# Two blocks at a time through the product with w_in, in the seven-product form of Strassen's method

## The chip, the cores and the metric

The kernel runs on one core of one Trainium2 chip. The metric is the device time of one execution in microseconds (us), the median of several. A core has TensorE (PE in the rows; its weight loads, which overlap the matmuls, are PEld), VectorE (DVE), ScalarE (ACT), GpSimd (POOL) and SyncE (SP), which here issues all DMAs. Each engine works through its own instructions in the order in which the program gave them; semaphores between engines say when one may start.

## What is computed

An attention in windows of 32 queries, and two multilayer perceptrons behind it, all in float32:

```python
x = attention(q, k, v, mem_k, mem_v)          # 3072 tokens x 512
h = np.maximum(np.maximum(x @ w1, x @ w2), x @ w3)   # 512 -> 768
x = h @ w_out_1                                # 768 -> 512
h = x @ w_in                                   # 512 -> 2048
g = np.where(h >= 1, h, np.where(h <= -1, 0.0, (h + 1) ** 2 / 4.0))
out = g @ w_out                                # 2048 -> 512
```

The change touches `x @ w_in` and what stands around it.

## The kernel before

**Blocks and products.** The 3072 tokens are NB = 6 blocks of 512. Every float32 operand of a product is split into a high part that TensorE takes at its full rate (`hi`, type fp32r) and the rest (`lo`), and each product is three matmuls: hi with hi, hi with lo, lo with hi (`mm3`, L483). ScalarE casts the high part, GpSimd or VectorE subtracts to get the low one (`split`, L498, for the values between layers).

**Slots.** Work is in slots of 12 matmuls, 128x128 stationary, 512 columns moving, 4 chunks x 3 terms. `slot_l1` and `slot_l2` are the first perceptron, `slot_l3(i, f)` (L576) is unit f (128 of the 2048 columns) of x @ w_in for block i, with the function g behind it: ScalarE's relu (L584), VectorE's min-multiply (L585) and maximum with the bank (L586), then `split` (L501, L503). `slot_l4(i, f)` (L589) adds that unit's share of the product with w_out in four banks; after unit 15 the banks are copied out and stored. In slot_l3 the weights are the stationary operand, in slot_l4 the moving one.

**Order.** The order is written out by hand. Up to some 150 us a list (`PLAN`) mixes loads, attention and the first block. Then a loop over `order` runs the first perceptron of blocks 1 to 5, 24 slots a block; up to block 4 one step of attention follows each slot, and in a cycle of six slots (`BY_PART`, L637, `round_step`, L617) the weights of the second perceptron are fetched, rounded on ScalarE and VectorE (`abs_w` to `sum_w`, L132 to L148) and stored to a buffer in DRAM, `wd`. In the last block (no attention left) `w_step` (L639) loads them back in pairs of units (L178) and splits them (`split_w`, L184 on ScalarE, L185 on VectorE). The order of the units is `round2` (L103): c0 c1, c2 d0, c3 d1, c4 d2 and so on, c for w_in and d for w_out. The first four pairs go into a pool `w2` of eight tiles at the right end of the memory, opened when attention's pool is closed (L724), the other twelve into `wpool`, tile by tile as the first perceptron's weights fall free. Last, `orderB` (L712 to L715) alternates slot_l4 of one unit with slot_l3 three units on, block after block, 96 of each. Its inputs, the first perceptron's results, come back from the DRAM buffer `yd` (`load_y`, L561) and are split for the next block during this one (`split_y`, L572 on ScalarE, L573 on GpSimd).

**Banks and tiles.** Banks 0 to 3 collect slot_l4 (and slot_l2), banks 6 and 7 take turns for slot_l1 and slot_l3. Tags in the pools say which tiles share buffers: `st` (two of 8 KB a partition) for fetched weights, `c` (two of 4 KB) for rounding, loads of y and outputs, `xh` and `xl` (two of 8 KB each) for a block's split input, `hh` and `hl` (three of 2 KB each) for split values between layers.

Of the kernel before, what the change touches and what calls it, by code (L numbers as in the profile page):

```python
# [65 lines left out]
def attention_then_two_mlps(ctx, tc, q, k, v, mem_k, mem_v, w1, w2, w3, w_mid, w_in, w_out, out):  # L66
# [25 lines left out]
    wd = dram.tile([2 * K2, P, TB], F32, name="wd")  # L92
# [14 lines left out]
    Q1, Q2 = len(round1) // 2, len(conv) // 2  # L107
# [39 lines left out]
    def sum_w(q, c):  # L147
        nc.vector.tensor_tensor(out=c, in0=c, in1=staged.pop(q)[:, :, :, 0], op=ALU.add)  # L148
# [382 lines left out]
    def slot_l2(j, f):  # L531
        hi, lo = hs.pop(("A", j, f))
        whi, wlo = weights["b", f]
        for d in range(KD):
            c = slice(d * P, (d + 1) * P)
            mm3(acc[d], whi[:, c], wlo[:, c], hi, lo, f == 0, f == K1 - 1)
            if f == K1 - 1:
                if bp:
                    y = pair_or_y(d < 2, f"y_{j}_{d}")
                else:  # L540
                    y = mx.tile([P, TB], F32, tag=("hh", "hl")[d % 2], name=f"y_{j}_{d}", bufs=3)
                nc.scalar.copy(out=y, in_=acc[d])
                store = partial(nc.sync.dma_start, out=yd[d * P:(d + 1) * P, j * TB:(j + 1) * TB], in_=y)
                if bp:
                    store()
                else:
                    stores.append(store)

    yr, yh, yl, halves = {}, {}, {}, []

    def pair_or_y(paired, name):
        if not paired:
            return mx.tile([P, TB], F32, tag="y", name=name, bufs=2)
        if not halves:
            t = stage.tile([P, 2, TB], F32, tag="c", name=name, bufs=2)
            halves.extend(t[:, i] for i in range(2))
        return halves.pop(0)

    def load_y(i, h):
        yr[i, h] = stage.tile([P, 2, TB], F32, tag="c", name=f"yr{i}_{h}", bufs=2)  # L560
        nc.sync.dma_start(  # L561
            out=yr[i, h],
            in_=yd[2 * h * P:2 * (h + 1) * P, i * TB:(i + 1) * TB].rearrange("(k p) t -> p k t", p=P))

    def split_y(i, h):
        if h == 0:
            yh[i] = mx.tile([P, KD, TB], F32R, tag="xh", name=f"yh{i}")
            yl[i] = mx.tile([P, KD, TB], F32R, tag="xl", name=f"yl{i}")
        src = yr.pop((i, h))
        for k in range(2):  # L570
            kk = 2 * h + k
            nc.scalar.copy(out=yh[i][:, kk, :], in_=src[:, k])  # L572
            nc.gpsimd.tensor_tensor(  # L573
                out=yl[i][:, kk, :], in0=src[:, k], in1=yh[i][:, kk, :].bitcast(F32), op=ALU.subtract)

    def slot_l3(i, f):  # L576
        s = next_mm()
        whi, wlo = weights["c", f]
        for kk in range(KD):
            c = slice(kk * P, (kk + 1) * P)  # L580
            mm3(s, whi[:, c], wlo[:, c], yh[i][:, kk, :], yl[i][:, kk, :], kk == 0, kk == KD - 1)

        a = mx.tile([P, TB], F32, tag="t", name=f"u_{i}_{f}", bufs=2)
        nc.scalar.activation(out=a, in_=s, func=AF.Relu, bias=0.5, scale=0.5)  # L584
        nc.vector.scalar_tensor_tensor(out=a, in0=a, scalar=1.0, in1=a, op0=ALU.min, op1=ALU.mult)  # L585
        nc.vector.tensor_tensor(out=a, in0=s, in1=a, op=ALU.max)  # L586
        split(("B", i, f), a, f"b{i}_{f}")

    def slot_l4(i, f):  # L589
# [3 lines left out]
        for t in range(TB // P):  # L593
# [4 lines left out]
            if last:  # L598
                ob = pair_or_y(t % 2, f"ob{i}_{t}")
# [10 lines left out]
    bp = {}  # L610
# [6 lines left out]
    def round_step(acts):  # L617
        if "out" in acts and kept:
            q, c = kept.pop(0)
            n = 2 * (q - Q1)  # L620
            nc.sync.dma_start(out=wd[n:n + 2].rearrange("t p f -> p t f"), in_=c)
# [5 lines left out]
        if "b" in acts and q in tiles:  # L627
            sum_w(q, tiles[q])
            kept.append((q, tiles.pop(q).bitcast(F32)))
# [7 lines left out]
    BY_PART = "out in in", "", "", "a", "", "b"  # L637

    def w_step(room):  # L639
# [4 lines left out]
        if room > 0 and q < asked[0]:  # L644
            split_w(q, bp["w"] if q < Q1 + 4 else wpool)
            ready[0] += 1

    with tc.manual_schedule(engines={ENG.PE, ENG.DVE, ENG.Activation, ENG.Pool, ENG.SP}):
# [63 lines left out]
        orderB = [(slot_l3, 0, 0), (slot_l3, 0, 1), (slot_l2, NB - 1, K1 - 1), (slot_l3, 0, 2)]  # L712
        l3 = [(slot_l3, i, f) for i in range(NB) for f in range(K2)]
        l4 = [(slot_l4, i, f) for i in range(NB) for f in range(K2)]
        orderB += [s for a, b in zip(l4, l3[3:] + [None] * 3) for s in (a, b) if s]  # L715

        last_block = 0
        for s, (f, *a) in enumerate(order):
            j = a[0]
            if f is not slot_l2 and j == NB - 1 and last_block == 0:  # L720
# [3 lines left out]
                bp["w"] = ctx.enter_context(tc.tile_pool(name="w2", bufs=8, side="right"))  # L724
# [14 lines left out]
            if last_block:  # L739
# [3 lines left out]
                w_step(t - 2 * (ready[0] - Q1 - 4) - 3)  # L743
                if t in (8, 14):
                    split_y(0, t // 6 - 1)
                if t in (2, 8):
                    load_y(0, t // 6)
# [8 lines left out]
        for s, (f, *a) in enumerate(orderB):  # L756
            w_step(s > 2)
            if f is slot_l3:
                i, ff = a
                assert ("c", ff) in weights and ("d", max(ff - 2, 0)) in weights  # L760
            f(*a)
            if f is slot_l3 and i + 1 < NB:
                if ff in (5, 9):
                    split_y(i + 1, ff // 4 - 1)
                if ff in (1, 5):
                    load_y(i + 1, ff // 4)
# [30 lines left out]
```

## Time and profile before

| | us |
|---|---|
| median of three runs | 1052.25 (1051.94 to 1056.75) |
| the profiled execution, its own time | 1055.15 |
| its span, first to last instruction | 1053.3 |

| engine | busy us | share of the span |
|---|---|---|
| PE | 1027.2 | 98% |
| DVE | 456.7 | 43% |
| ACT | 350.1 | 33% |
| POOL | 227.7 | 22% |

A matmul's record lasts from its start to a modelled end, and records of neighbours overlap; what a matmul costs in a full queue is the distance from its start to the next one's. Busy shares of the whole span mix stages, so the rows below are read stage by stage: the first 150 us or so are loads and attention, 157 to 452 us the middle stage (first perceptron and attention), 452 to 519 us the last block of the first perceptron, and from there the second perceptron.

### The profile page before, as it was taken

To read this page: it belongs to the slowest core of one execution; us is meant where nothing else is said; L and a number is where in the kernel's file an instruction comes from. 1 tells how busy PE (TensorE), PEld (TensorE's weight loads), DVE (VectorE), ACT (ScalarE), POOL (GpSimd) and SP (SyncE) were. 2 spreads that over 40 slices of the span, in tenths; PEclk is the share of its full clock that TensorE was granted. 3 is DMA by queue.
4 is the path that set the end of the run, shared out by engine and by line. 5 is a ranking of instruction groups with operands and counts; after the bars stand their busy time and mean duration, and the time that the engine had idled before them with its cause. 6 is when DMAs were issued, how large, how long until landed. Compare 5 with 4: busy or idle time off the path is not lost.

```text
span 1053.3 us, 17983 instructions
## 1 busy us (share of the span) xinstructions
PE 1027.2 (98%) x7542; PEld 832.3 (79%) x7542; DVE 456.7 (43%) x733; ACT 350.1 (33%) x545; POOL 227.7 (22%) x172
## 2 busy tenths in 40 slices
PE   7799899999999999999999999999999999999998
PEld 5677678878877878888888888888888888888886
DVE  4699934466565565534332232232222223223222
ACT  5665533342333332333332222222222222222222
POOL 0023410100000000103123223323322322332221
PEclk9999999999999999999999999999999999999999
DMA  7866547557456445154210010010001001001001
GB/s 166 216 166 172 142 122 199 123 120 198 113 125 200 114 111 178 38 189 151 100 61 21 1 60 21 1 54 26 1 1 61 21 1 60 1 1 40 1 1 40
DMA packets 163808, 89.91 MB, mean 85 GB/s; under 512 B 126096, under 2 KB 143504, under 8 KB 163728
## 3 DMA queue, kind: packets, MB, share of 16 engines
q1 hardware_dynamic: 163728, 88.77, 30.6%
q8 instruction: 59, 0.97, 0.4%
q14 instruction: 21, 0.17, 0.0%
HBM read 67.76 MB, written 20.97 MB: 84 GB/s over the span
## 4 chain that ended last, share of the span: by engine, by line
PE 87%; DVE 7%; DMA 3%; SPq 1%; issue 1%; ACT 1%; POOL 0%; DVEq 0%; POOLq 0%; ACTq 0%
PE bank L484 19%; PE bank L485 19%; PE bank L486 19%; PE bank L597 8%; PE bank L596 8%; PE bank L595 8%; DVE c L144 1%; PE bank L397 1%; DVE c L148 1%; PE bank L355 1%; DVE c L141 1%; SPq L243 1%; DMA kq<-in_k_dram 1%; DVE c L142 1%; PE bank L417 1%
## 5 line engine op out<-in xcount | busy, mean ns | idle before, releaser
L585 DVE SCALAR_TENSOR_TENSOR u<-u 128x512 f32<-128x512 f32 x96 | 71.2, 741 | 367.5 <-ACT u L584 367.5
L503 POOL TENSOR_TENSOR hl_b<-u,hh_b 128x512 fp32r<-128x512 f32 x96 | 123.8, 1290 | 373.9 <-ACT hh_b L501 256.0
L484 PE MATMUL bank<-xh,hi 128*128 128x512 f32 x432 | 174.9, 405 | 1.2 <-ACT xh L425 0.7
L486 PE MATMUL bank<-xh,lo 128*128 128x512 f32 x432 | 168.9, 391 | 1.8 <-POOL lo L173 1.8
L485 PE MATMUL bank<-xl,hi 128*128 128x512 f32 x432 | 169.0, 391 | 0.3 <-DVE xl L429 0.2
L484 PE MATMUL bank<-yh,hi 128*128 128x512 f32 x384 | 150.4, 392 | 0.0
L485 PE MATMUL bank<-yl,hi 128*128 128x512 f32 x384 | 150.2, 391 | 0.0
L486 PE MATMUL bank<-yh,lo 128*128 128x512 f32 x384 | 150.2, 391 | 0.0
L597 PE MATMUL bank<-hi,hl_b 128*128 128x512 f32 x384 | 150.0, 391 | 0.0
L596 PE MATMUL bank<-lo,hh_b 128*128 128x512 f32 x384 | 149.9, 390 | 0.0
L595 PE MATMUL bank<-hi,hh_b 128*128 128x512 f32 x384 | 149.8, 390 | 0.0
L584 ACT ACTIVATE u<-bank 128x512 f32<-128x512 f32 x96 | 57.6, 600 | 238.7 <-PE bank L486 220.1
L503 POOL TENSOR_TENSOR hl_a<-t,hh_a 128x512 fp32r<-128x512 f32 x34 | 47.0, 1382 | 338.2 <-ACT hh_a L501 292.3
L501 ACT CAST hh_b<-u 128x512 fp32r<-128x512 f32 x96 | 59.6, 621 | 147.8 <-DVE u L586 147.8
L486 PEld LDWEIGHTS bank<-xh,lo 128*128 128x128 f32 x432 | 81.1, 188 | 20.3 <-POOL lo L173 2.7
L484 PEld LDWEIGHTS bank<-xh,hi 128*128 128x128 f32 x432 | 81.2, 188 | 19.3 <-DVE t L519 1.2
L485 PEld LDWEIGHTS bank<-xl,hi 128*128 128x128 f32 x432 | 81.3, 188 | 15.9 <-DVE xl L429 1.0
L519 DVE TENSOR_TENSOR t<-bank,t 128x512 f32<-128x512 f32 x72 | 49.6, 689 | 85.7 <-PE bank L486 85.1
L485 PEld LDWEIGHTS bank<-yl,hi 128*128 128x128 f32 x384 | 72.2, 188 | 15.8
L486 PEld LDWEIGHTS bank<-yh,lo 128*128 128x128 f32 x384 | 72.1, 188 | 15.9
L484 PEld LDWEIGHTS bank<-yh,hi 128*128 128x128 f32 x384 | 72.1, 188 | 15.7
L595 PEld LDWEIGHTS bank<-hi,hh_b 128*128 128x128 f32 x384 | 72.1, 188 | 15.6
(88 smaller groups left out, 1247.0 us busy)
## 6 DMA issues: line engine op xcount, KB each, us to landing
st<-in_moe_w_out_dram SPq DMA_DIRECT2D x22, 512.0 KB
st<-in_moe_w_dram SPq DMA_DIRECT2D x18, 512.0 KB
vw<-in_v_dram SPq DMA_DIRECT2D x152, 56.0 KB
st<-in_moe_w_in_dram SPq DMA_DIRECT2D x16, 512.0 KB
wd<-c SPq DMA_DIRECT2D x16, 512.0 KB
w<-wd SPq DMA_DIRECT2D x16, 512.0 KB
yd<-y SPq DMA_DIRECT2D x24, 256.0 KB
yr<-yd SPq DMA_DIRECT2D x12, 512.0 KB
```

What stands on the lines that cost most here:

```text
L141: V.tensor_scalar(out=cf, in0=cf, scalar1=LEAST, scalar2=MOST, op0=ALU.max, op1=ALU.min)
L484: nc.tensor.matmul(out, whi, xhi, start=first, stop=False)
L485: nc.tensor.matmul(out, whi, xlo, start=False, stop=False)
L486: nc.tensor.matmul(out, wlo, xhi, start=False, stop=last)
L501: nc.scalar.copy(out=hi, in_=h)
L503: e.tensor_tensor(out=lo, in0=h, in1=hi.bitcast(F32), op=ALU.subtract)
L519: nc.vector.tensor_tensor(out=cur["t", j, f], in0=s, in1=cur["t", j, f], op=ALU.max)
L584: nc.scalar.activation(out=a, in_=s, func=AF.Relu, bias=0.5, scale=0.5)
L585: nc.vector.scalar_tensor_tensor(out=a, in0=a, scalar=1.0, in1=a, op0=ALU.min, op1=ALU.mult)
L595: nc.tensor.matmul(acc[t], hi[:, c], whi, start=first, stop=False)
L596: nc.tensor.matmul(acc[t], hi[:, c], wlo, start=False, stop=False)
L597: nc.tensor.matmul(acc[t], lo[:, c], whi, start=False, stop=last)
```

## The change

Two blocks j and j+1 (512 tokens each), the two halves of w_in's 512 rows and the pairs of units (n, n+8) make a 2x2 times 2x2 product. The seven-product form needs seven combinations of w_in's quarters, seven of y's, seven products of a 128x256 with a 256x512 matrix in place of eight, and seven additions of bank results.

- *Weights.* `round2` puts w_out's 16 units first, then w_in's as pairs (f, f+8). For w_in's eight pairs `combine_w` makes three combinations with four VectorE operations of 128x256 behind `sum_w`; the seven matrices of a pair go to a new DRAM buffer `cd` in two stores. The fetch of the next weights moves from part 0 of the six-slot cycle to part 2. Only w_out's eight pairs are loaded back and split, all into `wpool`; `w2` is gone.
- *Coefficients.* They are loaded from `cd` again for every pair of blocks, 4 + 3 of a unit pair at a time (`load_c`), into single tiles of a new pool `rp` that opens where `w2` did. `split_c` splits one 128x256 coefficient (ScalarE cast, GpSimd subtraction) into one of eight tiles `cs`, also in `rp`, and asks for the next load when a tile is used up.
- *Inputs.* `prep` loads the four quarters A to D of a pair's y, makes four differences, and splits seven operands (`split_y`: ScalarE cast, VectorE subtraction): for the first pair in the last block of the first perceptron (`LAST_BLOCK`, by slot), for the next pairs beside the second block's slot_l4 (`NEXT_PAIR`, by unit). b11 lies in `rp`, the others in buffers of `xh`, `xl` and `st`.
- *Products.* `pair_slot` runs seven products of 6 matmuls for one n, in turn over banks 4 to 7. VectorE adds them up; the four results are units n and n+8 of both blocks. Those of block j are split at once and used by slot_l4 one n later (`mid`); those of block j+1 are kept (`keep`, in `wpool`) and split when that block's 16 slot_l4 follow after n = 7. g's maximum now takes its input from a tile in memory where it took it from a bank.

The diff, cut to its core:

```diff
-    round2 = [("c", 0), ("c", 1), ("c", 2)]
-    for f in range(K2):
-        round2 += [("d", f)] + ([("c", f + 3)] if f + 3 < K2 else [])
+    round2 = [("d", f) for f in range(K2)] + [("c", f + h) for f in range(HF) for h in (0, HF)]
...
+    def combine_w(st, c):
+        d = st.bitcast(F32).rearrange("p a b c -> p (a b c)")[:, 0:3 * HK].rearrange("p (m f) -> p m f", m=3)
+        (a11, a12), (a21, a22) = [[c[:, i, k * HK:(k + 1) * HK] for k in range(2)] for i in range(2)]
+        sub = partial(nc.vector.tensor_tensor, op=ALU.subtract)
+        sub(out=d[:, 1], in0=a11, in1=a21)
+        nc.vector.tensor_tensor(out=a21, in0=a21, in1=a22, op=ALU.add)
+        sub(out=d[:, 0], in0=a21, in1=a11)
+        sub(out=d[:, 2], in0=a12, in1=d[:, 0])
+        return d
...
+    PRODUCTS = [(0, "b11"), (2, "t2"), (1, "b21"), (3, "t3"), (4, "t1"), (5, "t4"), (6, "b22")]
...
+    def split_c():
+        s = put[0]
+        if s >= limit[0]:
+            return
+        n, k = divmod(s, 7)
+        t = raw[2 * n + (k >= PARTS)][:, PRODUCTS[k][0] % PARTS]
+        cs[s] = c = rp.tile([P, 2, HK], F32R, tag="cr", name=f"cs{s}", bufs=8)
+        nc.scalar.copy(out=c[:, 0], in_=t)
+        nc.gpsimd.tensor_tensor(out=c[:, 1], in0=t, in1=c[:, 0].bitcast(F32), op=ALU.subtract)
+        put[0] += 1
+        if k in (PARTS - 1, 6) and loaded[0] < total // 7 * 2:
+            del raw[2 * n + (k >= PARTS)]
+            load_c(loaded[0])
+            loaded[0] += 1
+
+    def product(s, bank):
+        _, b = PRODUCTS[s % 7]
+        c = cs.pop(s)
+        for i in range(2):
+            r = slice(i * P, (i + 1) * P)
+            mm3(bank, c[:, 0, r], c[:, 1, r], mat[b][:, 0, i], mat[b][:, 1, i], i == 0, i == 1)
...
+    def g_relu(x, a):
+        nc.scalar.activation(out=a, in_=x, func=AF.Relu, bias=0.5, scale=0.5)
+
+    def g_rest(x, a):
         nc.vector.scalar_tensor_tensor(out=a, in0=a, scalar=1.0, in1=a, op0=ALU.min, op1=ALU.mult)
-        nc.vector.tensor_tensor(out=a, in0=s, in1=a, op=ALU.max)
-        split(("B", i, f), a, f"b{i}_{f}")
+        nc.vector.tensor_tensor(out=a, in0=x, in1=a, op=ALU.max)
...
+    def pair_slot(p, n, mid):
...
+        b = next_product(0)
+        c11 = mx.tile([P, TB], F32, tag="y", name=f"c11_{s}", bufs=2)
+        nc.scalar.copy(out=c11, in_=b)
+        split_c()
+        b = next_product(1)
...
+        add(out=c12, in0=b, in1=c11)
+        split_c()
+        mid(0)
+        b = next_product(2)
+        add(out=c11, in0=b, in1=c11)
...
+        g_relu(c11, a11)
+        split_c()
+        b = next_product(3)
...
+        add(out=c21, in0=b, in1=c12)
+        split_c()
+        b = next_product(4)
...
+        add(out=c22, in0=b, in1=c21)
+        add(out=c12, in0=b, in1=c12)
+        g_rest(c11, a11)
+        h22 = kept_h(n + HF)
+        g_relu(c22, h22)
+        split(("B", j, n), a11, f"b{j}_{n}")
+        split_c()
+        mid(1)
+        g_rest(c22, h22)
+        b = next_product(5)
+        add(out=c21, in0=b, in1=c21)
...
+        g_relu(c21, a21)
+        split_c()
+        if n == HF - 1:
+            g_rest(c21, a21)
+            split(("B", j, n + HF), a21, f"b{j}_{n + HF}")
+            mid(2)
+        b = next_product(6)
+        add(out=c12, in0=b, in1=c12)
+        h12 = kept_h(n)
+        g_relu(c12, h12)
+        if n < HF - 1:
+            g_rest(c21, a21)
+            split(("B", j, n + HF), a21, f"b{j}_{n + HF}")
+            split_c()
+            mid(2)
...
+        g_rest(c12, h12)
...
-    BY_PART = "out in in", "", "", "a", "", "b"
+    BY_PART = "out", "", "in in", "a", "", "b"
...
-            split_w(q, bp["w"] if q < Q1 + 4 else wpool)
+            split_w(q, wpool)
...
+        LAST_BLOCK = {0: "A B", 1: "C D", 5: "b11", 6: "T1", 7: "b22", 8: "T2", 9: "b21", 10: "T3", 11: "T4",
+                      12: "raw", 13: "raw", 15: "c", 16: "c", 17: "c", 18: "c", 20: "t2", 21: "t3"}
+        NEXT_PAIR = {0: "A B", 1: "C D", 4: "b11 T1", 5: "b22 T2", 6: "b21 T3", 7: "T4 t2", 8: "t3",
+                     9: "t1", 10: "t4", 11: "c c", 12: "c c", 13: "c c c"}
...
+        step["t1"]()
+        step["t4"]()
...
+            if n:
+                if i:
+                    slot_l4(j, n - 1 + HF * (i - 1))
+                if n == HF - 1 and i == 2:
+                    split_kept(j + 1, 0)
+                    slot_l4(j, n)
+                    split_kept(j + 1, 1)
+                    slot_l4(j, n + HF)
+            elif p:
+                if i:
+                    slot_l4(j - 1, K2 - 3 + i)
...
+            for f in range(K2 - 2 if more else K2):
+                if f + 2 < K2:
+                    split_kept(j + 1, f + 2)
+                slot_l4(j + 1, f)
```

## Rows read from the trace of the kernel before

**Rows 1.** The one core: its span and the mean granted TensorE clock.

```profile
core 0: 1053.3 us, clock 1.000
```

**Rows 2.** Stretches: busy us and (instructions) per engine, clock, DMA share, GB/s.

```profile
500.00:600.00 100.00, 100.00 (x439) 82.23 (x439) 32.22 (x40) 30.57 (x48) 26.86 (x22) 1.00 0.14 48
...
900.00:1000.00 100.00, 100.00 (x439) 82.26 (x438) 27.95 (x40) 25.38 (x43) 28.22 (x22) 1.00 0.03 11
```

**Rows 3.** TensorE in order of time (start, length, line, operands): the stage's ends.

```profile
519.55 0.39 PE L484 MATMUL bank<-yh,hi 128*128 128x512 f32 x1
...
1048.76 0.39 PE L597 MATMUL bank<-hi,hl_b 128*128 128x512 f32 x1
```

**Rows 4.** TensorE in order of time: slots' first matmuls, 12 matmuls apart, two places.

```profile
604.62 0.39 PE L484 MATMUL bank<-yh,hi 128*128 128x512 f32 x1
...
607.43 0.40 PE L595 MATMUL bank<-hi,hh_b 128*128 128x512 f32 x1
...
638.00 0.39 PE L484 MATMUL bank<-yh,hi 128*128 128x512 f32 x1
...
640.72 0.39 PE L595 MATMUL bank<-hi,hh_b 128*128 128x512 f32 x1
```

**Rows 5.** By source line: count, duration in ns (least/median/most); first a page's group.

```profile
L585 DVE SCALAR_TENSOR_TENSOR u<-u 128x512 f32<-128x512 f32 x96 | 71.2, 741 | 367.5 <-ACT u L584 367.5
...
L585 DVE SCALAR_TENSOR_TENSOR u<-u x96: 678/694/1244, 523.3 to 1041.7; 128x512 f32<-128x512 f32 x96
L519 DVE TENSOR_TENSOR t<-bank,t x72: 680/692/694, 59.2 to 519.8; 128x512 f32<-128x512 f32 x72
L185 DVE TENSOR_TENSOR lo<-w,hi x16: 1216/1226/2253, 458.9 to 535.8; 128x1024 fp32r<-128x1024 f32 x16
L372 DVE TENSOR_TENSOR p<-bank,m x48: 423/424/426, 13.1 to 434.3; 128x256 f32<-128x256 f32 x48
L584 ACT ACTIVATE u<-bank x96: 598/599/628, 522.6 to 1041.1; 128x512 f32<-128x512 f32 x96
L501 ACT CAST hh_b<-u x96: 619/622/624, 524.7 to 1043.2; 128x512 fp32r<-128x512 f32 x96
L517 ACT COPY t<-bank x36: 558/586/592, 56.4 to 511.6; 128x512 f32<-128x512 f32 x36
L184 ACT CAST hi<-w x16: 1047/1051/1079, 457.8 to 534.7; 128x1024 fp32r<-128x1024 f32 x16
L503 POOL TENSOR_TENSOR hl_b<-u,hh_b x96: 1283/1288/1300, 525.5 to 1043.9; 128x512 fp32r<-128x512 f32 x96
```

**Rows 6.** A w load's issue, the cast that waited for it, SP's waits for stores.

```profile
460.12 0.36 SPq L178 DMA_DIRECT2D w<-wd  x1
...
464.09 1.05 ACT L184 CAST hi<-w 128x1024 fp32r<-128x1024 f32 x1 [1.01 <-DMA w<-wd]
...
SPq L561 <- DMA out_dram<-ob: 9.0, 4, 2.3
```

**Rows 7.** Stretches of 20 us (columns as in rows 2): last block, and a quiet one.

```profile
460.00:480.00 20.00, 20.00 (x89) 16.39 (x88) 8.53 (x10) 9.07 (x13) 1.94 (x2) 1.00 0.67 222
480.00:500.00 20.00, 20.00 (x90) 16.55 (x89) 8.55 (x8) 7.61 (x11) 8.56 (x7) 1.00 0.42 146
...
560.00:580.00 20.00, 20.00 (x90) 16.58 (x89) 5.24 (x7) 5.33 (x9) 7.65 (x6) 1.00 0.00 1
```

**Rows 8.** Middle stage: TensorE from 157 to 452 us, then VectorE, then the gap.

```profile
sum 295.00, PE 293.44; mean PE 19.56
...
318.03 0.69 DVE L519 TENSOR_TENSOR t<-bank,t 128x512 f32<-128x512 f32 x1 [1.15 <-PE bank L486]
320.65 0.69 DVE L519 TENSOR_TENSOR t<-bank,t 128x512 f32<-128x512 f32 x1 [1.93 <-PE bank L486]
326.07 0.71 DVE L333 STREAM_TRANSPOSE kw<-kq 128x512 f32<-128x512 f32 x1 [4.73 <-DMA kq<-in_k_dram]
...
331.82 0.66 PE L417 MATMUL bank<-ident,xs 128*128 128x128 f32 x4 [1.56 <-DVE xs L410]
```

More of the change, by code (lines that the diff above doesn't have):

```diff
@@ L565, in split_y @@
[L565 to L584, printed above, removed]
-        nc.vector.scalar_tensor_tensor(out=a, in0=a, scalar=1.0, in1=a, op0=ALU.min, op1=ALU.mult)
-        nc.vector.tensor_tensor(out=a, in0=s, in1=a, op=ALU.max)
-        split(("B", i, f), a, f"b{i}_{f}")
+    OPERANDS = "b11 b21 b22 t1 t2 t3 t4".split()
@@ new lines, in halves_of, with split_y @@
+    def halves_of(y):
+        return [y[:, i] for i in range(2)] if not isinstance(y, list) else y
+    def split_y(name, y):
+        if name not in mat:
+            mat[name] = new_mat(name)
+        t = mat[name]
+        for hi, lo, x in zip(halves_of(t[:, 0]), halves_of(t[:, 1]), halves_of(y)) if isinstance(y, list) else (
+                (t[:, 0], t[:, 1], y),):
+            nc.scalar.copy(out=hi, in_=x)
+            nc.vector.tensor_tensor(out=lo, in0=x, in1=hi.bitcast(F32), op=ALU.subtract)
@@ L742, in attention_then_two_mlps @@
                 round_step(["out"])
[L743 to L747, printed above, removed]
+                w_step(t - 2 * (ready[0] - Q1) - 3)
+                for name in LAST_BLOCK.get(t, "").split():
+                    if name == "c":
+                        split_c()
+                    elif name == "raw":
+                        load_c(loaded[0])
+                        loaded[0] += 1
+                    else:
+                        step[name]()
             else:
@@ L755, in attention_then_two_mlps, with keep_h, split_kept, between @@
             l1_split(*x)
[L756 to L766, printed above, removed]
+        step["t1"]()
+        step["t4"]()
+        def keep_h(n):
+            while len(keep) < n:
+                keep.append(wpool.tile([P, 2, TB], F32, tag="w", name=f"h{len(keep)}"))
+        def split_kept(j, f):
+            split(("B", j, f), kept_h(f), f"b{j}_{f}")
+        def between(p, n, i):
+            j = 2 * p
+            if n:
[9 more added lines that the diff above has]
+                    slot_l4(j - 1, K2 - 3 + i)
+            elif i == 0:
+                keep_h(HF - 2)
+                for _ in range(3):
+                    split_c()
+            elif i == 1:
+                slot_l2(NB - 1, K1 - 1)
+                keep_h(HF)
+        for p in range(NB // 2):
+            j = 2 * p
+            for n in range(HF):
+                pair_slot(p, n, partial(between, p, n))
+            more = p + 1 < NB // 2
+            step = prep(p + 1) if more else {}
+            if more:
+                limit[0] += HF * 7
+            for f in range(K2 - 2 if more else K2):
+                if f + 2 < K2:
+                    split_kept(j + 1, f + 2)
+                slot_l4(j + 1, f)
+                for name in NEXT_PAIR.get(f, "").split():
+                    if name == "c":
+                        split_c()
+                    elif step:
+                        step[name]()
 _INS = ['q', 'k', 'v', 'mem_k', 'mem_v', 'moe_w1', 'moe_w2', 'moe_w3', 'moe_w_out', 'moe2_w_in', 'moe2_w_out']
```

122 lines of the change are left out of this document (89 added, 33 removed).

## The prediction

> **What bounds the kernel now.** I read the span and clock first: one core, 1053.3 us, and the granted clock is 1.000 of full speed, the 2.4 GHz level, throughout [rows 1]. Then busy time by stage: from 500 us to 1000 us TensorE is busy all of each 100 us, while VectorE has 28 to 32 us of work, ScalarE 25 to 31 and GpSimd 27 to 28 [rows 2] (the first and the last of five such rows). So nothing but TensorE sets the end there, and work of the other engines is free as long as its turn comes in time. Third, the stage itself: the first product with w_in starts at 519.55 us, the last matmul of all at 1048.76 [rows 3]. Between them lie 1152 matmuls of the w_in product, 1152 of the w_out product, and 12 of one slot_l2.
>
> The records of these matmuls last 391 ns each, but that is not what one costs: they overlap. The cost is the distance of their starts, and it has two values. A slot of 12 takes 2.72 us (638.00 to 640.72, 0.2267 us each) in most places, and 2.81 us (604.62 to 607.43, 0.2342 us each) in others [rows 4]. In every 16+16 slots of a block eight are slow: w_in's units 0 to 4 and w_out's 0 to 2. These are exactly the units that w_step splits first, the four pairs that go into the pool `w2` at the right end of the memory (L724); all others lie in `wpool`. It is the same whether the weight is the stationary operand (slot_l3) or the moving one (slot_l4). I take it that an operand in that region costs 0.0075 us a matmul more. Check: 6 blocks x (8 x 2.81 + 24 x 2.72) = 526.5, and 2.7 for slot_l2, gives 529.2 us; rows 3 have 529.4 to the end of the last start step (1048.76 + 0.23 - 519.55).
>
> **What it removes.** The 1152 matmuls of slot_l3: 6 x (5 x 2.81 + 11 x 2.72) = 263.8 us. **What it adds.** Per pair of blocks and per n 7 products x 2 halves of the contraction x 3 terms = 42 matmuls; 3 pairs x 8 x 42 = 1008. Form and count per instruction are those of slot_l3 (128x128 stationary, 512 columns). Their stationary operand `cs` lies in the pool `rp`, which stands where `w2` stood (33 KB a partition for 32). At 0.2342 us they cost 236.0, at 0.2267 us 228.5. I take 236.0, by the slow slots; the b11 products have both operands there, and at twice the surcharge would add 144 x 0.0075 = 1.1 us. **What moves.** w_out's units all go to `wpool`: its product falls from 6 x (3 x 2.81 + 13 x 2.72) = 262.7 to 96 x 2.72 = 261.1. Sum on TensorE: 526.5 - 497.1 = **29.4 us less** (36.9 with fast products).
>
> The Trainium skill (TensorE: Matmul & The Clock Gate, "Back-to-back issue gap") gives N/2.4 + 2.5 ns, 216 ns for 512 columns, with no word on where an operand lies. By it the gain would be 144 x 0.216 = 31.1 us. Rows 4 are 5 and 8% above it and show two values, so the rows decide.
>
> **Does the other work keep up?** A middle pair_slot (42 product matmuls, two slot_l4) lasts 42 x 0.2342 + 24 x 0.2267 = 15.3 us on TensorE. Against that, from [rows 5]:
> - VectorE: 7 additions with a bank at 0.69, 4 min-multiplies at 0.69 and 4 maxima at 0.69: 10.4 us.
> - ScalarE: one bank copy 0.59, 4 relus 0.60, 2 casts 0.62, 7 casts of 128x256. No row has that cast; between 0 and 0.62 (128x512), I take 0.41 from the line through 0.62 and 1.05 (128x1024). Sum 7.1 us, at most 8.6.
> - GpSimd: 2 subtractions of 128x512 at 1.29 and 7 of 128x256, between 0 and 1.29 each, of which I take 0.7, a little over half of 1.29: 7.5 us, at most 11.6.
>
> All end below 15.3, so per slot they cost nothing if order doesn't hold TensorE. In order: a bank is reused four products on, 5.5 us later, and the copy or addition that frees it is queued at once; after product 4, VectorE has two additions and 4 of the 8 g operations ahead of product 5's addition, 4.1 us of work, under the 2.72 of slot_l4 and product 5's own 1.40. The coefficients run seven products ahead. The value a21 of one n is wanted a whole slot later. A coefficient load is issued about 10 us before its first cast; a 512 KB load took 3.6 us from its issuing start (460.12) to the cast that waited for it (464.09, with 1.0 us of wait) [rows 6]. I charge 0, and 0 to 1 us for each last n (n = 7), where slot_l4(j, 15) comes only two slots after product 5 while a21 needs 0.69 + 0.60 + 0.69 + 0.69 + 0.62 + 1.29 = 4.6 us: three times, 0.5 us in all.
>
> The second block's 16 slot_l4 follow without products between: 2.72 us each against 0.62 + 1.29 for its split, two slots ahead. Beside them VectorE has 11 operations of 128x1024 at 1.22 = 13.4 us for the next pair's operands in 38 us. Here SP and the DMA queue come in: load A waits for the stores of the block just finished (in the kernel before such loads waited for them up to 2.3 us [rows 6]), then A, B, C and D, 2 MB behind 1 MB of stores, must land by step 6, some 18 us on. 3 MB in 18 us is 170 GB/s; the busiest 20 us of this stage moved 222 [rows 7]. A late landing stops ScalarE, behind it the next splits, and after the 5 us that these run ahead, TensorE. Bounds 0 to 5 us, twice; I take 0.5.
>
> **The last block of the first MLP** loses eight w loads and gets A to D, two coefficient loads, seven operand splits, four subtractions: beside 24 slots of 2.72 us VectorE and ScalarE were busy for 7.6 to 9.1 us of each 20 [rows 7], so it fits. But SP issues w loads, A, B, C, D and four y stores within 20 us, about 4 to 5 MB, just what the rows show as the most. Late operands stop ScalarE's bank copies. 0 to 6 us; I take 1. At the passage, t1 and t4 are split only after the last slot_l1 (ScalarE 2.4 us, VectorE 2.8), under four products of 5.6 us, with c11's copy behind them: 0 to 1, I take 0.5.
>
> **The middle stage**, 157 to 452 us, is TensorE-bound too; it lost 1.56 us in one place, where a late kq load held VectorE for 4.73 us [rows 8]. There combine_w adds eight times four operations of 128x256, at 0.42 (same shape, one input in a bank) 1.7 us, behind the sum. Hidden by VectorE's waits of 1.15 and 1.93 us for TensorE in the two slots after such a sum [rows 8]; without that cover 8 x 1.7 = 13.6 us. The fetches move from part 0 to part 2, behind the y stores and some queue entries; they get the kq loads out earlier, but for w_in each now waits for its tile's two stores, and v loads queue behind. -1.6 to +5 us; I take 0.5. The tail after the last matmul, 4.5 us, stays.
>
> **Sum.** -29.4 + 0.5 + 0.5 + 1 + 0.5 + 0.5 = -26.4 us. The profiled run took 1055.15 us with a span of 1053.3, 2.9 us above the median of the runs, 1052.25; I carry the difference over: 1055.15 - 26.4 = 1028.8 for such a run, **1026 us** as a median.
>
> **Rivals.** (a) *The products run at 0.2267 us*: the surcharge then isn't the place but something of the old weight tiles. For it: no row shows a 1 KB tile there. Against it: eight slots of each block go by the pool. 1026 - 7.5 = 1018.5, down to 1014 if the other charges vanish. (b) *Landings hold ScalarE at the passages*: the bounds of A to D (10), the last block (6) and the middle (5) in part: 1031 to 1042. Against it: between such places the DMA engines stand idle, at 0.00 from 560 to 580 us [rows 7], so that nothing else is in their way. (c) *VectorE and GpSimd shut each other out, and VectorE becomes the bound*: ends on the other side. After the change eight of VectorE's 15 operations per slot have both inputs in memory, against one in three before, and GpSimd is busy 7.5 of 15.3 us instead of a quarter. The rows show such waits: the min-multiply goes from 0.68 to 1.24 us, the 128x1024 subtraction from 1.22 to 2.25 [rows 5]. It decides where the eight wait over (15.3 - 10.4)/8 = 0.6 us on average. If each waits out a whole GpSimd operation (mean 7.5/9 = 0.83 us), VectorE has 17.0 us a slot, 1.7 over, 24 times: 1026 + 41 = 1067 us, slower. Against it: the mean min-multiply is 0.74 [rows 5], 0.05 over its median, so at twice the GpSimd share some 0.1 each.
>
> The Trainium skill states this rule (SBUF — State Buffer, "SBUF: two separate sides"): a VectorE operation with two SBUF inputs and a GpSimd operation hold the shared port in turn, and the loser waits for the whole instruction. The trace agrees in kind; its longest wait for that row is 0.55 us.
>
> (d) *The gain is given back in several places and nothing is left*: waits of over 21 us with no single cause.
>
> **Chances.** The forecast (1021 to 1031) 0.55; (a) 0.20; (b) 0.14; (c) 0.05; (d) 0.06, of which 0.04 within 0.5% and 0.02 slower. About 0.5%, 5 us, is what a measurement of this kernel can tell from no change. Faster: 0.55 + 0.20 + 0.14 = 0.89; same 0.04; slower 0.07. The range takes in (a) to 1014 and the near half of (b) to 1037: some 0.82.
>
> **What would show it.** Right: 1008 records of the product line with starts 0.234 us apart, slot_l4 at 0.227 everywhere, TensorE busy all of each 100 us after the first products, VectorE near 70% in the pair slots. (a) shows as 0.227 in the products. (b) shows as ScalarE waiting for a DMA with TensorE idle behind it, at the two passages between pairs or in the last block. (c) shows as VectorE busy throughout, its g operations at 1.2 us and more, and TensorE waiting for bank releases in every n. Wrong altogether: a TensorE gap that comes back in each of the 24 slots.

## The result and the profile after

| | before | after |
|---|---|---|
| median of the runs | 1053.51 us (1051.94 to 1056.75) | 1023.61 us (1022.64 to 1025.25) |
| ratio after/before | | 0.9714, 95% interval 0.9685 to 0.9743 |
| the profiled run, and its span | 1055.15, 1053.3 us | 1023.47, 1021.7 us |
| TensorE busy in the span | | 999.6 us, 98% |
| VectorE, ScalarE, GpSimd busy in the span | | 633.9, 418.2, 355.7 us |

The change makes the kernel 2.9% faster, about 30 us. The forecast was 1026.0 us, range 1014 to 1037. The clock of after, beside [rows 1]:

```profile
core 0: 1021.7 us, clock 0.998
```

Stretches of after (window, its length, then busy us and instructions of TensorE, its weight loads, VectorE, ScalarE, GpSimd; clock, DMA share, GB/s): the middle stage, one that answers the first of [rows 2], one middle pair slot, and 14 w_out slots in a row.

```profile
157.00:452.00 295.00, 295.00 (x3149) 236.48 (x3148) 183.64 (x347) 97.71 (x146) 30.96 (x23) 1.00 0.55 147
500.00:600.00 100.00, 100.00 (x434) 81.18 (x433) 67.92 (x94) 45.26 (x97) 56.04 (x57) 1.00 0.22 67
...
560.20:575.50 15.30, 15.30 (x67) 12.40 (x66) 10.33 (x16) 6.48 (x14) 8.87 (x9) 1.00 0.21 61
642.20:680.30 38.10, 38.10 (x170) 31.56 (x169) 24.48 (x20) 18.50 (x32) 24.28 (x18) 1.00 0.19 66
```

TensorE is still busy all of the time, in the middle stage too, where it had lost 1.56 us before [rows 8]. The other engines do much more beside it: from 500 to 600 us VectorE works 68 us, where it did 32.

TensorE of after in order of time (start, length, line, operands), for [rows 3, 4]: the first product, a middle pair slot with 30 product matmuls, 12 of slot_l4 and the next product, and the last matmul.

```profile
517.01 0.40 PE L496 MATMUL bank<-b,cs 128*128 128x512 f32 x1
...
560.20 0.40 PE L496 MATMUL bank<-b,cs 128*128 128x512 f32 x1
...
567.21 0.40 PE L730 MATMUL bank<-hi,hh_b 128*128 128x512 f32 x1
...
569.97 0.39 PE L496 MATMUL bank<-t,cs 128*128 128x512 f32 x1
...
1017.39 0.39 PE L732 MATMUL bank<-hi,hl_b 128*128 128x512 f32 x1
```

The 30 products take 7.01 us, 0.234 each; the 12 of slot_l4 2.76, 0.230 each, and 0.227 where 14 slots follow each other (168 matmuls in 38.09 us). From the first product to the end of the last start step the stage lasts 1017.39 + 0.23 - 517.01 = 500.6 us, where before had 529.4. So the span's 31.6 us divide into 28.8 in the stage, 2.5 ahead of it (519.55 to 517.01), and 0.3 in the tail.

The lines of after that took over from [rows 5] (count, then least/median/most ns):

```profile
L656 DVE SCALAR_TENSOR_TENSOR a<-a x48: 680/682/1299, 526.2 to 966.4; 128x512 f32<-128x512 f32 x48
L657 DVE TENSOR_TENSOR a<-c,a x48: 691/695/1115, 527.6 to 967.1; 128x512 f32<-128x512 f32 x48
...
L515 POOL TENSOR_TENSOR hl_b<-a,hh_b x48: 1294/1694/1752, 529.0 to 968.7; 128x512 fp32r<-128x512 f32 x48
...
L586 POOL TENSOR_TENSOR cs<-ra,cs x96: 725/739/1717, 498.2 to 944.9; 128x256 fp32r<-128x256 f32 x96
```

VectorE's least times are the old ones, and so are its medians. It is GpSimd's split of `a` that is drawn out, from a median of 1.29 to 1.69 us.

### The profile page after: what moved, and what is told of

It is laid out like the page before. It is cut to its first block, busy times and chain, and to the rows that moved or that the text cites. A ratio compares the mean times of both kernels' runs of the same rounds, so it can differ in the third digit from the quotient of the medians.

```text
span 1021.7 us, 18724 instructions
## 1 busy us (share of the span) xinstructions
PE 999.6 (98%) x7398; PEld 806.7 (79%) x7398; DVE 633.9 (62%) x976; ACT 418.2 (41%) x735; POOL 355.7 (35%) x316
## 4 chain that ended last, share of the span: by engine, by line
PE 88%; DVE 8%; DMA 2%; issue 1%; SPq 1%; ACT 1%; POOL 0%; DVEq 0%; POOLq 0%; ACTq 0%
PE bank L496 19%; PE bank L497 19%; PE bank L498 19%; PE bank L730 9%; PE bank L731 9%; PE bank L732 9%; DVE c L144 2%; DVE c L149 1%; PE bank L409 1%; PE bank L367 1%; DVE c L141 1%; DVE c L142 1%; PE bank L429 1%; DMA st<-in_moe_w_dram 1%; PE bank L395 1%
## 5 line engine op out<-in xcount | busy, mean ns | idle before, releaser
L515 POOL TENSOR_TENSOR hl_b<-a,hh_b 128x512 fp32r<-128x512 f32 x48 | 80.4, 1675 | 119.1 <-ACT hh_b L513 119.1
L515 POOL TENSOR_TENSOR hl_b<-h,hh_b 128x512 fp32r<-128x512 f32 x48 | 68.1, 1421 | 51.5 <-ACT hh_b L513 51.4
L586 POOL TENSOR_TENSOR cs<-ra,cs 128x256 fp32r<-128x256 f32 x96 | 73.7, 789 | 33.7 <-ACT cs L585 33.7
L732 PEld LDWEIGHTS bank<-hi,hl_b 128*128 128x128 f32 x384 | 72.1, 188 | 15.5
L731 PEld LDWEIGHTS bank<-lo,hh_b 128*128 128x128 f32 x384 | 72.1, 188 | 15.1
L497 PE MATMUL bank<-t,cs 128*128 128x512 f32 x192 | 76.1, 396 | 0.0
L496 PE MATMUL bank<-t,cs 128*128 128x512 f32 x192 | 76.0, 396 | 0.0
L498 PE MATMUL bank<-t,cs 128*128 128x512 f32 x192 | 76.0, 396 | 0.0
L653 ACT ACTIVATE a<-c 128x512 f32<-128x512 f32 x48 | 30.4, 633 | 90.8 <-DVE c L683 54.2
L586 POOL TENSOR_TENSOR cs<-rb,cs 128x256 fp32r<-128x256 f32 x72 | 63.3, 882 | 10.3 <-ACT cs L585 9.2
```

The lines of the kernel that those rows point to most:

```text
L496: nc.tensor.matmul(out, whi, xhi, start=first, stop=False)
L497: nc.tensor.matmul(out, whi, xlo, start=False, stop=False)
L498: nc.tensor.matmul(out, wlo, xhi, start=False, stop=last)
L515: e.tensor_tensor(out=lo, in0=h, in1=hi.bitcast(F32), op=ALU.subtract)
L586: nc.gpsimd.tensor_tensor(out=c[:, 1], in0=t, in1=c[:, 0].bitcast(F32), op=ALU.subtract)
L653: nc.scalar.activation(out=a, in_=x, func=AF.Relu, bias=0.5, scale=0.5)
```

## The experiments

Two theories had to be told apart at each of three steps: what makes a product cost 0.234 us; what the moved fetch is worth; and how near VectorE and GpSimd stand to becoming the bound. The runs came in batches, and the median of the kernel before moved between 1053.5 and 1054.9 us from one to the next; so a difference of one or two microseconds between medians says little, and the traces are read beside them.

**1. The coefficients in another place.** The weights of the products go from the pool `rp` to tiles of `wpool`; to make room, the kept h tiles go to the right end.

```diff
-        cs[s] = c = rp.tile([P, 2, HK], F32R, tag="cr", name=f"cs{s}", bufs=8)
+        if len(cw) <= s // 2 and s < 8:
+            cw.append(wpool.tile([P, 2, 2, HK], F32R, tag="w", name=f"cw{s // 2}"))
+        cs[s] = c = cw[s // 2 % 4][:, s % 2]
...
+                keep.extend(rp.tile([P, 2, TB], F32, tag="k", name=f"h{i}", bufs=4) for i in range(4))
```

> The split coefficients (the products' stationary operand) move from the pool at the right end into four wpool tiles; four of the eight kept-value tiles go to the right end instead. Instruction counts stay. Theory: the extra 0.0075 us of a product matmul (0.2342 against 0.2267 us from start to start) comes with the place of an operand. Then 864 of the 1008 product matmuls fall to 0.227 us, those of b11, which stays at the right end and is now the only operand there, stay at 0.232 to 0.234, and the time falls by 864 x 0.0075 = 6.5 us to about 1017 us. Rival: the products are slow by their form (tiles of 1 KB, a new accumulation every six matmuls); then all stay at 0.234 us and the time at 1023.6.

Measured: 1018.80 us, ratio to before 0.965 (0.9629 to 0.967). TensorE in order of time, one b11 product (its moving operand is still in `rp`), the t2 product behind it, and its end:

```profile
561.55 0.40 PE L496 MATMUL bank<-b,cw 128*128 128x512 f32 x1
...
562.96 0.39 PE L496 MATMUL bank<-t,cw 128*128 128x512 f32 x1
...
564.35 0.39 PE L496 MATMUL bank<-b,cw 128*128 128x512 f32 x1
```

The b11 product takes 1.41 us, 0.235 a matmul, as slow as ever. The last four of the seven products run at 0.2267 to 0.2277 on average over the stage. The stage is 5.8 us shorter (494.8 us), for 6.5 expected. The second and third product, t2 and b21, are only partly quicker: 0.2321 and 0.2286 on average. They follow the slow one, and run 2 shows that this is why.

**2. b11 too.** On top of 1, b11 goes into the two `c` buffers of the pool `stage`, whose other users go to the right end instead.

```diff
-            return rp.tile([P, 2, 2, TB], F32R, tag="ym", name=name)
+            return [stage.tile([P, 2, TB], F32R, tag="c", name=f"{name}{x}", bufs=2) for x in "hl"]
...
-            v[name] = y = stage.tile([P, 2, TB], F32, tag="c", name=f"{name}_{p}", bufs=2)
+            v[name] = y = rp.tile([P, 2, TB], F32, tag="y2", name=f"{name}_{p}", bufs=2)
```

> As the run with the coefficients in wpool, and b11 moves too, into the two buffers of tag c; the loads A and C and the output tiles take its place at the right end. Theory of the place: all 1008 product matmuls at 0.227 us, another 1.1 us less than with the coefficients alone, about 1016 us. If only the stationary operand's place counts, no difference between the two. Rival of the form: 0.234 us everywhere, 1023.6.

Measured: 1016.40 us, ratio 0.9632 (0.9607 to 0.9657). TensorE in order of time:

```profile
559.92 0.39 PE L496 MATMUL bank<-t,cw 128*128 128x512 f32 x1
...
565.37 0.39 PE L733 MATMUL bank<-hi,hh_b 128*128 128x512 f32 x1
...
568.09 0.39 PE L496 MATMUL bank<-t,cw 128*128 128x512 f32 x1
```

24 matmuls of products in 5.45 us, 0.2271 each; 12 of slot_l4 in 2.72. Averaged over the stage all seven products are at 0.2267 to 0.2296. The stage is 7.7 us shorter than after's, where 7.6 was expected. Form, count and order of the matmuls are unchanged: the surcharge goes with the place of an operand, stationary or moving, and not with the products' form. The operands of t2 and b21 lie where they lay in run 1, and both products are now at 0.2267. So a slow product also delays the starts of some matmuls behind it: in run 1 the three products from b11 on took 1.41, 1.39 and 1.37 us in nearly every n. What makes that end of the memory slower is open. Of the kernels that compute the whole result this is the fastest, 37 us below before.

**3. The change with the fetches left in part 0.**

```diff
-    BY_PART = "out", "", "in in", "a", "", "b"
+    BY_PART = "out in in", "", "", "a", "", "b"
```

> The changed kernel with the weight fetches back in part 0 of the six-slot cycle, as before the change. Theory: the first product starts 2.5 us earlier after the change (517.01 for 519.55 us), because the fetches leave the queue free for the attention's kq load that held VectorE for 4.73 us; put back, the gap of about 1.6 us in the middle stage returns, the first product starts at about 519 us or later, and the time is 1025 to 1027. Rival: the earlier start comes from the order of the units (w_out first); then nothing changes here.

Measured: 1032.66 us, ratio 0.9777 (0.9753 to 0.9802): 9 us slower than after, more than either theory gave. The stage itself lasts as long as after's (500.6 us); the loss lies ahead of it. The queue SP in order of time around the stores of combine_w (start, length, line, transfer), in after:

```profile
315.50 0.35 SPq L760 DMA_DIRECT2D cd<-c  x1
316.45 0.35 SPq L761 DMA_DIRECT2D cd<-st  x1
...
319.67 2.27 SPq L750 DMA_DIRECT2D kq<-in_k_dram  x4
```

The same queue at the same stores in this experiment:

```profile
317.78 0.35 SPq L760 DMA_DIRECT2D cd<-c  x1
318.73 0.35 SPq L761 DMA_DIRECT2D cd<-st  x1
321.46 0.94 SPq L120 DMA_DIRECT2D st<-in_moe_w_in_dram  x2
...
325.00 3.52 SPq L750 DMA_DIRECT2D kq<-in_k_dram  x4
```

The fetch of `st` waits for the store from the same tile (318.73 + 0.35 to 321.46), and everything queued behind it comes late: kq is issued at 325.00 instead of 319.67. VectorE and TensorE of this experiment in order of time:

```profile
330.79 0.71 DVE L345 STREAM_TRANSPOSE kw<-kq 128x512 f32<-128x512 f32 x1 [7.62 <-DMA qs<-in_q_dram]
...
331.70 0.39 PE L498 MATMUL bank<-xh,lo 128*128 128x512 f32 x1
336.53 1.11 PE L429 MATMUL bank<-ident,xs 128*128 128x128 f32 x4 [4.45 <-DVE xs L422]
...
338.29 0.63 PE L498 MATMUL bank<-xh,lo 128*128 128x512 f32 x1
338.72 0.63 PE L496 MATMUL bank<-xh,hi 128*128 128x512 f32 x1
```

The same two matmuls in after, where TensorE doesn't stand:

```profile
329.39 0.39 PE L498 MATMUL bank<-xh,lo 128*128 128x512 f32 x1
329.62 0.66 PE L429 MATMUL bank<-ident,xs 128*128 128x128 f32 x4
```

TensorE's stretches in the experiment (window, its length, then busy us and instructions, clock, DMA share, GB/s):

```profile
337.00:340.00 3.00, 3.00 (x10) 0.50 0.44 86
340.00:343.00 3.00, 3.00 (x57) 0.63 0.73 224
343.00:346.00 3.00, 3.00 (x43) 1.00 0.44 173
```

VectorE stands 7.62 us for the load, TensorE 4.45 us for VectorE, and then the granted clock is 0.50 of full speed, the 1.2 GHz level. Ten matmuls in a row start 0.427 us apart, which costs (0.427 - 0.227) x 10 = 2.0 us more. Matched matmul by matmul, the experiment's TensorE runs 2.3 us behind after's just ahead of the place (331.70 beside 329.39), 6.9 us at the transposes (336.53 beside 329.62) and 9.5 us where the clock is back. So this one place costs 7.2 us. Some 1.5 of the 2.3 us arose at 131 us, where the clock also stood at 0.50 for a few matmuls; runs 7 and 10, with after's program up to there, show such a fall as well, runs 5, 6 and 9 none, so it can't be put down to the fetches.

**4. The kernel before with the fetches in part 2 alone.**

```diff
-    BY_PART = "out in in", "", "", "a", "", "b"
+    BY_PART = "out", "", "in in", "a", "", "b"
```

> The kernel before with the fetches alone moved to part 2, nothing else. Theory: the middle stage's gap goes and the time falls by about 2 us to 1051. Rival (order of the units): no change, 1053.

Measured: 1053.53 us, ratio 0.9991 (0.9971 to 1.0011). A gain of the expected size can't be told from none in these runs. In the trace the wait of [rows 8] is gone:

```profile
321.70 0.71 DVE L333 STREAM_TRANSPOSE kw<-kq 128x512 f32<-128x512 f32 x1 [0.75 <-DMA qs<-in_q_dram]
```

0.75 us stand where 4.73 stood, with no gap of TensorE behind it, and over this place the run's matmuls gain 1.7 us on those of before, where some 2 were expected. The time is inconclusive; the mechanism is seen. Read with run 3: in the kernel before, the gap behind the late load was 1.56 us [rows 8]; in the changed kernel without the move it is 4.45 us, with a fall of the clock behind it. combine_w's operations now stand ahead of the stores; that this is the whole reason was not tested.

**5. Six products.** The matmuls of the seventh product are left out.

```diff
-        b = next_product(6)
-        add(out=c12, in0=b, in1=c12)
+        cs.pop(s + 6)
+        add(out=c12, in0=banks[4 + (s + 6) % 4], in1=c12)
```

> The changed kernel without the matmuls of product 6 (the one with b22): its coefficient is still split and the addition still reads the bank, with what product 2 left there, so the work of the other engines stays; part of x @ w_in is left out. 24 x 6 = 144 matmuls fewer. Theory (TensorE alone sets the pace of the pair slots, other engines fit): 144 x 0.2342 = 33.7 us less, about 990 us, as a pair slot falls from 15.3 to 13.9 us with VectorE at 10.3. Rival (the pair slots are already held by VectorE or GpSimd in their order): clearly less than 33.7 us.

This kernel leaves out a part of x @ w_in. Measured: 989.17 us, ratio 0.9384 (0.9361 to 0.9407): 34.4 us less than after. 144 matmuls at 0.2342 are 33.7. In the trace the stage lost 32.7 of them (467.9 us), with one new wait of TensorE, 0.97 us in the second slot. TensorE alone sets the pace at the change's load, and what is taken from it comes back nearly whole.

**6. Five more operations on VectorE per n.** They have one memory tile as both inputs and change no value.

```diff
+        for _ in range(5):
+            V.tensor_tensor(out=c11, in0=c11, in1=c11, op=ALU.max)
```

> Five more VectorE operations of 128x512 with both inputs in memory at the end of each pair slot (c11 = max(c11, c11), the values are not used afterwards). VectorE then has 10.3 + 5 x 0.69 = 13.8 us of work in 15.3. Theory (it fits as long as its work stays under TensorE's slot): no change, 1023.6 us within 2. Rival (waits between VectorE and GpSimd make VectorE the bound): 18 to 24 waits more, VectorE over 15.3 us a slot, and 10 to 40 us slower.

Measured: 1074.3 us, ratio 1.0199 (1.0169 to 1.0229): 50.7 us slower than after, slower than before too, and more than the 40 of the rival. My theory fell. VectorE in order of time:

```profile
568.21 0.69 DVE L657 TENSOR_TENSOR h<-c,h 128x512 f32<-128x512 f32 x1
568.82 5.94 DVE L724 TENSOR_TENSOR c<-c 128x512 f32<-128x512 f32 x5
574.89 0.69 DVE L679 TENSOR_TENSOR c<-bank,c 128x512 f32<-128x512 f32 x1
```

GpSimd in the same stretch:

```profile
568.37 1.68 POOL L515 TENSOR_TENSOR hl_b<-a,hh_b 128x512 fp32r<-128x512 f32 x1 [1.34 <-ACT hh_b L513]
570.00 1.19 POOL L586 TENSOR_TENSOR cs<-rb,cs 128x256 fp32r<-128x256 f32 x1
571.15 2.33 POOL L586 TENSOR_TENSOR cs<-ra,cs 128x256 fp32r<-128x256 f32 x2
```

All 120 of the added operations (least/median/most ns):

```profile
L724 DVE TENSOR_TENSOR c<-c x120: 679/1111/1789, 533.5 to 1032.9; 128x512 f32<-128x512 f32 x120
```

The five take 1.19 us each where 0.69 was counted, while GpSimd works through four operations without a pause, and those too are longer than the least times (1.68 for 1.29, 1.17 for 0.73). Most slots grow to 17.65 us (15.31 in after), and TensorE waits 19 times, 27.3 us, for the addition of L679 behind them. Put together: from 568.37 to 574.76, 6.39 us, the two engines do what at their least times is 5 x 0.69 + 1.29 + 3 x 0.73 = 6.93 us. Side by side it would have been 3.5 us. So they do these operations nearly in turn.

**7. Nine more** (the same line with `range(9)`).

> Nine more such operations: 10.3 + 9 x 0.69 = 16.5 us of VectorE work in a slot of 15.3. Theory: now VectorE is over by 1.2 us in each of 24 slots; some of it is taken up by the banks at the start and by the stretch of 16 slot_l4 behind each pair, so 15 to 30 us slower, 1039 to 1054. If it stays at 1023.6, the sum of operation times is not the measure.

Measured: 1135.43 us, ratio 1.0776 (1.0753 to 1.0798): 112 us slower than after, where 15 to 30 were expected. One slot, 552 to 572.5 us (columns as in the first stretches):

```profile
552.00:572.50 20.50, 17.09 (x67) 13.46 (x66) 19.09 (x24) 6.35 (x15) 9.84 (x10) 0.92 0.15 45
```

VectorE is busy 19.09 of 20.5 us: it is the bound. The four operations beyond five cost 61 us over 24 slots, 0.64 each, about the plain price. GpSimd's work is over by then: in this slot it ends at 560.24, VectorE's nine operations at 564.42, the last five of them 0.69 us each, and GpSimd starts again only at 567.15:

```profile
567.15 1.42 POOL L586 TENSOR_TENSOR cs<-ra,cs 128x256 fp32r<-128x256 f32 x2 [6.90 <-ACT cs L585]
```

**8. GpSimd's coefficient subtraction done twice.**

```diff
-        nc.gpsimd.tensor_tensor(out=c[:, 1], in0=t, in1=c[:, 0].bitcast(F32), op=ALU.subtract)
+        for _ in range(2):
+            nc.gpsimd.tensor_tensor(out=c[:, 1], in0=t, in1=c[:, 0].bitcast(F32), op=ALU.subtract)
```

> GpSimd makes each coefficient's subtraction twice: 8.9 + 7 x 0.74 = 14.0 us of work in a slot of 15.3. Theory: no change, 1023.6 us within 3, VectorE's two-input operations lengthen a little. Rival (VectorE and GpSimd shut each other out): VectorE's maxima and min-multiplies grow from a mean of 0.7 to 0.9 us to over 1.2, its slot passes 15.3 us, and the time grows by 10 us and more.

Measured: 1051.95 us, ratio 0.9975 (0.9965 to 0.9984): 28.3 us slower than after, nearly the whole gain. The theory of no change fell. Some 16 us of the second pair, where most slots last 16.3 to 16.5 us, and TensorE's longest entry in the list of waits (us in all, times, longest):

```profile
756.00:772.00 16.00, 15.15 (x66) 11.99 (x65) 12.63 (x15) 6.28 (x14) 15.45 (x17) 1.00 0.19 59
...
PE bank L496 <- ACT c L676: 17.2, 16, 4.9
```

GpSimd is busy 15.45 of 16.0 us, VectorE 12.63 for work that took 10.33. ScalarE waits for GpSimd's splits (its relu 101.8 us in 24 waits, in after 36.6 in 23), and TensorE for ScalarE's copy of a bank behind them. Seven subtractions at 0.74 would have made 8.87 + 5.2 = 14.1, under the slot of 15.3; the lengthened prices (0.92 on average) make the difference. So the rival's time came, but with GpSimd as the bound: of VectorE's min-multiplies only those of the kept tiles passed 1.2 us (median 1.22), the others stayed at 0.69.

**9. Three more operations on VectorE** (as 6, with `range(3)`).

> Three more two-input VectorE operations of 128x512 at the end of each pair slot, in place of five. With five, each took 1.19 us beside GpSimd's subtractions, and VectorE's chain filled the whole slot of 17.65 us with only 0.65 us of waits. Theory: what counts is whether VectorE's chain, at these lengthened prices, stays under TensorE's 15.3 us. Three give 17.65 - 2 x 1.19 = 15.3 us with the waits, at the edge: 1023.6 to 1030 us. Rival (any work put at the end of the slot delays the chain of the next n, whatever the sum): 3/5 of the 50 us that five cost, about 1054 us.

Measured: 1036.19 us, ratio 0.9824 (0.9791 to 0.9858): 12.6 us slower than after. VectorE:

```profile
564.68 4.07 DVE L724 TENSOR_TENSOR c<-c 128x512 f32<-128x512 f32 x3
```

1.36 us each. The time lies between the two theories. TensorE: the two longest waits at the end of the first pair, and two starts of the second pair's slots:

```profile
638.90 0.50 PE L734 MATMUL bank<-hi,hl_b 128*128 128x512 f32 x1 [1.07 <-POOL hl_b L515]
643.13 0.50 PE L734 MATMUL bank<-hi,hl_b 128*128 128x512 f32 x1 [0.68 <-POOL hl_b L515]
...
700.33 0.40 PE L496 MATMUL bank<-b,cs 128*128 128x512 f32 x1
...
715.63 0.40 PE L496 MATMUL bank<-b,cs 128*128 128x512 f32 x1
```

The loss isn't spread evenly. Six slots of the first pair last 15.66 to 15.79 us, 0.4 to 0.5 over after's 15.31, which makes 2.7 us. The slots of the second and third pair are 15.31, as if nothing had been added. The other 10.7 of the stage's 13.4 us are lost at the ends of the three pairs, 3.4 to 3.7 us each: there the last n's w_out slots wait for GpSimd's split, twice at each end.

**10. Five more, with a bank as one input.**

```diff
+        for _ in range(5):
+            V.tensor_tensor(out=c11, in0=b, in1=c11, op=ALU.max)
```

> Five more VectorE operations at the same place with product 6's bank as the first input, so one input in memory where the earlier five had two (c11 = max(bank, c11), not used afterwards). Theory (the price comes from two inputs in memory beside GpSimd's subtractions): each takes 0.69 us, the chain is 10.3 + 3.4 us and some waits, under 15.3, and the time is 1023.6 to 1030 us. Rival (the price comes from the place, at the end of the slot, or from the sum of VectorE's work): 1074 us as before with five.

Measured: 1053.29 us, ratio 0.998 (0.9963 to 0.9997). All 120 of the added operations (least/median/most ns):

```profile
L724 DVE TENSOR_TENSOR c<-bank,c x120: 676/691/692, 535.4 to 1010.2; 128x512 f32<-128x512 f32 x120
```

TensorE at the next product:

```profile
572.54 0.47 PE L496 MATMUL bank<-t,cs 128*128 128x512 f32 x1 [0.52 <-DVE c L724]
```

All 120 take 0.69 us, 107 of them while GpSimd works, and GpSimd isn't lengthened by them either; its two subtractions from `ra`, 1.17 us each in run 6:

```profile
570.71 1.43 POOL L586 TENSOR_TENSOR cs<-ra,cs 128x256 fp32r<-128x256 f32 x2
```

That the lengthening needs two inputs in memory is shown. The time fell between both expectations for a reason of the experiment: the five hold the bank that the next product wants, and TensorE waits for it 21 times, 19.9 us in all. That is two thirds of the 29.7 us over after.

## Why the forecast held, step by step

**TensorE's sum** (29.4 us less): right. The stage lost 28.8. Priced by start distances, it was to last 497.1 + 2.7 = 499.8 us; it lasted 500.6. What is over is in slot_l4, 0.2277 us on average over all of them for 0.2267 [rows 4]; behind products a slot takes 2.73 to 2.76 us, and with the products' operands moved (run 2) 2.72 again. That is the delay behind slow matmuls, which the sum didn't have. It was there before as well: w_in's unit 5, which lies in `wpool`, took 2.76 us in every block, behind a slow slot of w_out.

**The place of the operand**: right, and shown by runs 1 and 2, so rival (a) falls. Its pitch was to be had, but by moving tiles, for 7 us. One detail was wrong: b11 with both operands in the region pays the surcharge once, not twice (0.2324 us on average, beside 0.2330 to 0.2347 for the others).

**The charges** (3.0 us): too high, each of them. TensorE has no gap over 0.1 us from 157 us to the end, so the last n's, the passages between pairs, the last block and t1/t4 cost nothing. Rival (b) didn't come. From 157 us on, ScalarE's list of waits has one entry for a DMA, and none for the loads A to D. It is at its casts from `ra` (count, busy us and mean ns, idle time before and what ended it):

```profile
L585 ACT CAST cs<-ra 128x256 fp32r<-128x256 f32 x96 | 34.0, 402 | 1.4 <-DMA ra<-cd 1.4
```

It waits for loads 1.4 us in 96 casts, and one takes 0.40 us, where 0.41 was taken for want of a row.

**The middle stage**: taken at +0.5, it gave back 2.5 us in the two profiled runs, outside the bounds of -1.6 to +5. The wait I read [rows 8] did shrink, and TensorE has no gap left in it:

```profile
323.23 0.71 DVE L345 STREAM_TRANSPOSE kw<-kq 128x512 f32<-128x512 f32 x1 [2.38 <-DMA kq<-in_k_dram]
```

At this place before had started its matmuls 0.5 us behind after's ahead of the gap (329.87 beside after's 329.39) and 2.2 us behind it (331.82 [rows 8] beside 329.62), so 1.7 of the 2.5 us belong to the gap whose 1.6 I had set as the bound:

```profile
329.87 0.39 PE L486 MATMUL bank<-xh,lo 128*128 128x512 f32 x1
```

The rest came in steps under 0.2 us that I can't explain, and one profile against one doesn't settle it: in runs 5, 6, 7, 9 and 10, whose program is after's up to there, the first product starts anywhere from 515.5 to 517.8 us. What I failed to price was the other side: combine_w with the fetches *not* moved. Run 3 puts that at 9 us by the medians and at 7.2 by the trace, so of the edits outside the products that were tried apart this line is the one that matters.

**The other engines**: of what a slot was to hold, VectorE came to 10.33 us for 10.4, ScalarE to 6.48 for 7.1, GpSimd to 8.87 for 7.5. GpSimd is over mostly because its two splits of `a` take 1.69 and 1.75 us, not 1.29 [rows 5]; of the seven coefficients one took 1.20 us, the others 0.73 to 0.74 where 0.7 was taken.

**Rival (c)** named the right mechanism, and it doesn't decide at this load. The order keeps most of VectorE's two-input operations clear of GpSimd's: their median is 0.69. But the step "all end below 15.3, so per slot they cost nothing" gave a false margin. By it VectorE had 4.9 us left, seven operations of 0.69. Run 9 shows that three already cost 12.6 us, most of it at the ends of the pairs, and run 6 has TensorE wait for VectorE in 19 of the 24 slots with five. So a sum per slot was the wrong measure twice: the prices in it change when the engines meet, and the last n has less room than the other slots. The price under contention, half a microsecond more per operation in run 6, is close to the 0.6 us at which the rival was to decide. That the rival didn't decide here was foreseen, but the reason (a mean only 0.05 over the median in [rows 5]) was a weak one: that mean came from a kernel in which the two engines seldom met.

The Trainium skill (SBUF — State Buffer, "SBUF: two separate sides") has the two hold the shared port in turn, where VectorE's operation has two SBUF inputs. Runs 6 and 10 agree in the main: 6.93 us of work took 6.39 with two inputs in memory, and none of the added operations is lengthened with one in a bank.

**The final sum**: 1026.0 us for 1023.6 measured. By the spans the change was worth 31.6 us where 26.4 were worked out: 2.5 more from charges that didn't come, 3.0 from the middle stage (2.5 back instead of 0.5 lost), 0.3 in the tail, less 0.6 of TensorE's sum. The medians stand closer to the forecast than the spans, because the profiled run of before was 2.9 us over the median of the runs known then (1055.15 beside 1052.25), and that of after stands at its own (1023.47 beside 1023.61). So part of the 31.6 us belongs to that one run of before, and that 1026.0 came within 2.4 us is in part luck: by the spans the sum was 5.2 us off.

Two readings of the prediction were off, and neither the sum nor a chance hung on them. From the start of the w load's issue to the cast that waited for it [rows 6] it is 4.0 us (460.12 to 464.09); 3.6 is counted from the issue's end. And of VectorE's operations in the stage of before nearly every second one had both inputs in memory (96 of some 207), not one in three.

## What to carry to other kernels

Price a matmul by the distance of its starts, separately for every place where its operands lie; that alone gave the stage within 1 us, and moving the operands gave 7.7 us more. Where VectorE takes both inputs from memory while GpSimd works, count room in a slot at the lengthened price (1.2 us for 0.69) before calling it free, and count it where the order leaves least (here the ends of the pairs). Look at each DMA that a queue holds behind a wait: moving two fetches a few entries down was worth 7 to 9 us, about a quarter of the gain or more.

## What the runs showed of the hardware that was not expected

- The start distance of a 512-column matmul is 0.2267 us with no operand in the tiles at the right end, about 0.234 with one of them there, whichever operand it is, and no more with both (0.232, beside 0.235 for b11 alone there). Matmuls behind such slow ones are delayed too, though their own operands lie elsewhere (1.39 and 1.37 us for six, where 1.36 is the quick time; 2.76 for twelve, where 2.72 is).
- A VectorE operation with two memory inputs goes from 0.69 to 1.11 us (median), 1.79 at most, beside GpSimd, which is lengthened as well (0.73 to 1.17 us for 128x256): the two nearly take turns. With one input in a bank VectorE stays at 0.69 in all 120, and GpSimd at 0.73.
- After TensorE had stood 4.45 us, the granted clock was 0.50 (the 1.2 GHz level) and matmuls started 0.427 us apart, until it was 1.00 again from 343 us.
